# Moving the last third of a weight load to a second DMA queue in a pointwise-convolution kernel

## The chip, the cores and the metric

The kernel runs on one core of one Trainium2 chip. The metric is device time in microseconds (us), the median of several runs. "The profile" is one profiled execution of the same program; its span is counted from its first to its last instruction and is about 2 us shorter than the device time.

Engines are named as in the profile: PE is TensorE's matmul, PEld its weight load, DVE VectorE, ACT ScalarE, POOL GpSimd, SP SyncE. SPq and ACTq are the DMA issues of SyncE and ScalarE. [...]q1 is the queue of SyncE's transfers, q10 that of ScalarE's.

## The reference, cut to what matters

The input x has shape (1, 384, 384, 384), dw (1, 1, 384), pw (384, 384), all bf16.

```python
def reference(x, dw, pw):
    B, H, W, C = x.shape
    k = dw.shape[0]            # 1: no padding, no neighbours
    ...
    out = out + xp[:, i:i+H, j:j+W, :] * dw[i, j][None, None, None, :]
    return jnp.einsum('bhwc,cd->bhwd', out, pw)
```

With k = 1 each of the 147,456 pixels is a row of 384 channels, scaled by dw and multiplied by the 384 x 384 matrix pw.

## The kernel before

The scale is folded into the weights once, at the start: the kernel forms diag(dw) times pw by matmuls with scaled selection matrices (`sel_w`), which also puts the rows of pw into the order in which VectorE's 32 x 32 block transpose delivers the channels of x. The result is `w_r`. Then 288 tiles of 512 pixels each are transposed by VectorE, multiplied by TensorE (48 matmuls of 32 rows and 384 columns, four of them side by side in the array), cast by ScalarE and stored by SyncE.

The loads at the start. `pw_n` is a part of the tile `raw`, which is the name that the profile gives to it:

```python
nc.scalar.dma_start(dw_row[:], dw.rearrange("a e c -> a (e c)")).then_inc(s_dw, 16)
nc.sync.dma_start(pw_n[:, 0], pw[0:P, :]).then_inc(s_pw, 16)                       # line 178
nc.sync.dma_start(pw_n[:, 1:3], pw[P:C, :].rearrange("(k p) d -> p k d", p=P)).then_inc(s_pw2, 16)   # line 179
load_x(0)                                                                          # line 132: x0, 384 KB
# ... then x1 (384 KB), x2 and x3 (768 KB each), x4 (1536 KB), all on SyncE's queue;
# the first load of 3840 KB waits until x1 has landed
```

TensorE's program up to the main matmuls. The idle work keeps the array busy while nothing has arrived; the last third of the weights (k = 2) is multiplied twice for the same reason:

```python
idle_work(4)                                    # line 239, on constants
nc.tensor.wait_ge(s_dw, 16)
# ... three small matmuls that turn dw into a column
idle_work(2)
nc.tensor.wait_ge(s_pw, 16)
times = {(2, 0): 2, (2, 1): 2}
for k in range(3):
    if k == 1:
        nc.tensor.wait_ge(s_pw2, 16)
    nc.tensor.wait_ge(s_sw, k + 1)
    for r in range(2):
        if k == 2:
            nc.tensor.wait_ge(*w_done[r])       # PSUM free: the cast of step r is done
        for v in [0, 1] * times.get((k, r), 1):
            mm = nc.tensor.matmul(              # line 272
                PS[(k + 1) % 2][:, 2 * r + v, :D],
                lhsT=sel_w[64 * v : 64 * v + 64, k, r, :, :].rearrange("p q w -> p (q w)"),
                rhs=pw_n[64 * v : 64 * v + 64, k, :],
                start=True, stop=True, tile_position=(64 * v, 0),
            )
        mm.then_inc(s_w)
```

The six results are cast to `w_r`, the second by VectorE and the others by ScalarE (line 377, `w_out`). The main matmuls (line 222) wait for the transposed x and, in the first tile, for the casts as they need them:

```python
w_eng = [1, 0, 1, 1, 1, 1]                      # 0: VectorE, 1: ScalarE
w_first = {(0, 0): [(0, 1), (1, 3)], (4, 0): [(1, 4)], (4, 1): [(1, 5)]}
steps = [(b, par) for b in range(4) for par in range(2)] + [(4, 0), (5, 0), (4, 1), (5, 1)]
```

ScalarE's program begins with the issue of the dw load, then two small copies, then the casts:

```python
for s in range(2):
    nc.scalar.copy(warm[:, s : s + 1], nc.const_aps.tensor(0.0, [P, 1], F32)).then_inc(s_a[s])   # line 338
# ...
o = nc.vector.tensor_copy(out, in_) if e == 0 else nc.scalar.copy(out, in_)                      # line 377
```

## Time and profile before

| what | value |
|---|---|
| device time, median of 3 runs | 573.81 us (573.74 to 574.17) |
| span of the profile | 571.9 us |
| PE busy | 567.0 us (99%) |
| DVE busy | 505.4 us (88%) |
| ACT busy | 418.4 us (73%) |
| DMA, mean over the span | 397 GB/s |
| first main matmul (line 222) starts | 6.52 us |
| last main matmul of line 222 ends | 566.37 us |

A row of the groups view reads: line, engine, operation, tile written from tile read, shape, count, then busy time in us and the mean of one instruction in ns, then the idle time of the engine just before them and what ended most of it. A row of the chain view is start, length and what was running, for the chain of work that ended last. A row of the timeline is start and length in us, engine, line and operation, with the idle time ahead of it and what ended it in square brackets. A row of the DMA queues is queue, packets, MB and the time of the packets as a share of the 16 engines.

### The profile page before, as it was taken

To read this page: it belongs to the slowest core of one execution; us is meant where nothing else is said; L and a number is where in the kernel's file an instruction comes from. 1 tells how busy PE (TensorE), PEld (TensorE's weight loads), DVE (VectorE), ACT (ScalarE), POOL (GpSimd) and SP (SyncE) were. 2 spreads that over 40 slices of the span, in tenths; PEclk is the share of its full clock that TensorE was granted. 3 is DMA by queue.
4 is the path that set the end of the run, shared out by engine and by line. 5 is a ranking of instruction groups with operands and counts; after the bars stand their busy time and mean duration, and the time that the engine had idled before them with its cause. 6 is when DMAs were issued, how large, how long until landed. Compare 5 with 4: busy or idle time off the path is not lost.

```text
span 571.9 us, 29705 instructions
## 1 busy us (share of the span) xinstructions
PE 567.0 (99%) x13843; PEld 380.0 (66%) x13843; DVE 505.4 (88%) x586; ACT 418.4 (73%) x298; POOL 13.9 (2%) x41
## 2 busy tenths in 40 slices
PE   9999999999999999999999999999999999999997
PEld 4666666666666666666666666666666666666664
DVE  6889889889889889889889889889889889889885
ACT  6777777777777777777777777777777777777775
POOL 2042000000000000000000000000000000000000
PEclk9999999999999999999999999999999999999999
DMA  8999999999999999999999999999999999998677
GB/s 328 445 393 414 426 416 428 437 426 411 430 416 420 388 396 432 388 390 396 433 382 396 418 415 408 397 416 414 395 403 428 387 394 402 420 393 351 285 287 263
DMA packets 26740, 226.88 MB, mean 397 GB/s; under 512 B 1385, under 2 KB 7274, under 8 KB 22890
## 3 DMA queue, kind: packets, MB, share of 16 engines
q1 hardware_dynamic: 25796, 225.91, 97.4%
q10 hardware_dynamic: 934, 0.89, 0.4%
q14 instruction: 9, 0.07, 0.0%
q8 instruction: 1, 0.02, 0.0%
HBM read 113.54 MB, written 113.25 MB: 397 GB/s over the span
## 4 chain that ended last, share of the span: by engine, by line
PE 98%; DMA 1%; SPq 0%; DVE 0%; issue 0%; ACT 0%; POOLq 0%
PE ps L222 98%; DMA X<-in_x_dram 1%; PE ps L307 0%; PE ps L295 0%; DVE T L361 0%; ACT O L416 0%; SPq L179 0%; SPq L178 0%; SPq L457 0%; POOLq L112 0%; POOLq L446 0%
## 5 line engine op out<-in xcount | busy, mean ns | idle before, releaser
L222 PE MATMUL ps<-w_r,T 32*128 32x384 bf16 x13776 | 559.8, 321 | 0.2 <-DVE T L361 0.2
L361 DVE STREAM_TRANSPOSE T<-X 128x384 uint32<-128x384 uint32 x572 | 498.1, 874 | 58.2 <-DMA X<-in_x_dram 2.1
L421 ACT CAST O<-ps 128x1536 bf16<-128x1536 f32 x286 | 411.4, 1438 | 147.0 <-PE ps L222 147.0
L222 PEld LDWEIGHTS ps<-w_r,T 32*128 32x128 bf16 x13776 | 377.2, 93 | 183.1 <-issue 0.9
L336 POOL COPY Xk<-Xl 32x256 bf16<-32x256 bf16 x16 | 6.3, 394 | 0.0
L335 POOL COPY Xk<-Xl 32x128 bf16<-32x128 bf16 x16 | 4.6, 287 | 25.2 <-DMA Xl<-in_x_dram 24.3
L377 ACT CAST w_r<-ps 128x768 bf16<-128x768 f32 x5 | 3.6, 820 | 0.8 <-PE ps L272 0.8
L330 POOL COPY raw<-w_r 32x768 bf16<-32x768 bf16 x4 | 3.3, 819 | 6.4 <-ACT w_r L377 6.2
L239 PE MATMUL ps<-const-bfloat16-1.0 32*128 32x384 bf16 x24 | 2.2, 516 | 1.1 <-PEq L446 1.1
L272 PE MATMUL ps<-raw 64*128 64x384 bf16 x16 | 2.9, 513 | 0.1
L338 ACT ACT_TABLE_LOAD x1 | 1.3, 1283 | 1.5 <-PEq L446 1.5
L272 PEld LDWEIGHTS ps<-raw 64*128 64x128 bf16 x16 | 0.8, 113 | 2.2 <-DMA raw<-in_pw_dram 1.2
L412 DVE CAST O<-ps 128x384 bf16<-128x384 f32 x2 | 1.0, 552 | 1.4 <-PE ps L222 1.4
L361 DVE STREAM_TRANSPOSE T<-Xl 128x384 uint32<-128x384 uint32 x2 | 1.8, 876 | 0.2
L239 PEld LDWEIGHTS ps<-const-bfloat16-1.0 32*128 32x128 bf16 x24 | 0.7, 117 | 1.4 <-issue 1.4
L349 DVE STREAM_TRANSPOSE T<-Xk 128x384 uint32<-128x384 uint32 x2 | 1.2, 578 | 0.5 <-PE ps L222 0.4
L382 DVE TENSOR_REDUCE sel<-eye 128x64 f32<-128x128 bf16 x1 | 0.3, 290 | 1.5 <-POOL eye L317 1.5
L307 PE MATMUL ps<-raw,T 128*128 128x384 bf16 x8 | 1.5, 327 | 0.0
L416 ACT CAST O<-ps 128x384 bf16<-128x384 f32 x2 | 1.0, 478 | 0.7 <-PE ps L307 0.7
L377 DVE CAST w_r<-ps 128x768 bf16<-128x768 f32 x1 | 1.0, 958 | 0.5 <-PE ps L272 0.5
L416 DVE CAST O<-ps 128x384 bf16<-128x384 f32 x2 | 1.1, 558 | 0.1
L411 ACT CAST O<-ps 128x384 bf16<-128x384 f32 x2 | 0.9, 482 | 0.5 <-PE ps L222 0.5
(13 smaller groups left out, 4.5 us busy)
## 6 DMA issues: line engine op xcount, KB each, us to landing
X<-in_x_dram SPq DMA_DIRECT2D x26, 3840.0 KB, 21.9
out_dram<-O SPq DMA_DIRECT2D x26, 3840.0 KB, 27.9
X<-in_x_dram SPq DMA_DIRECT2D x3, 1536.0 KB, 18.5
out_dram<-O SPq DMA_DIRECT2D x4, 768.0 KB, 7.7
out_dram<-O SPq DMA_DIRECT2D x2, 1536.0 KB, 13.7
X<-in_x_dram SPq DMA_DIRECT2D x1, 2304.0 KB, 20.2
out_dram<-O SPq DMA_DIRECT2D x1, 2304.0 KB, 11.1
X<-in_x_dram SPq DMA_DIRECT2D x4, 384.0 KB, 4.4
```

What stands on the lines that cost most here:

```text
L222: mm = nc.tensor.matmul(PS[s][:, q, :D], lhsT=Ts[s][32 * q : 32 * q + 32, b, par::2], rhs=w_r[32 * q : 32 * q + 32, b, par, :], start=(b, ...
L239: nc.tensor.matmul(PS[0][:, 2 * (i % 2) + i // 2, :D], lhsT=ones[32 * i : 32 * i + 32, 0:P], rhs=ones[32 * i : 32 * i + 32, :], start=True ...
L272: mm = nc.tensor.matmul(PS[(k + 1) % 2][:, 2 * r + v, :D], lhsT=sel_w[64 * v : 64 * v + 64, k, r, :, :].rearrange("p q w -> p (q w)"), rhs ...
L307: mm = nc.tensor.matmul(PS[1][:, m, :D], lhsT=Tk[:, P * (m + 2) : P * (m + 3), par], rhs=w_k[:, par, :], start=False, stop=par == 1,)
L330: nc.gpsimd.tensor_copy(w_k[quads[n]], w_r[quads[n], n]).then_inc(s_wk)
L335: nc.gpsimd.tensor_copy(Xk[quads[n], g:8:4, :], x_b).then_inc(s_xk)
L336: nc.gpsimd.tensor_copy(Xk[quads[n], 8 + g : 24 : 4, :], Xl[quads[g], :, 64 * n : 64 * n + 64]).then_inc(s_xk)
L338: nc.scalar.copy(warm[:, s : s + 1], nc.const_aps.tensor(0.0, [P, 1], F32)).then_inc(s_a[s])
L361: ins = nc.vector.transpose(out=Tw[:, 3 * h : 3 * h + 3], in_=Xw[:, :, j, 96 * h : 96 * h + 96].rearrange("p k (b w) -> p b k w", w=32),)
L377: o = nc.vector.tensor_copy(out, in_) if e == 0 else nc.scalar.copy(out, in_)
L416: o = (nc.scalar.copy if n % 2 else nc.vector.tensor_copy)(Ov[:, n, j, :], PS[s][:, n, :D])
L421: a = nc.scalar.copy(Ov[:, :, j, :], PS[s][:, :, :D])
```

## The change

pw is loaded in three parts of 128 rows (96 KB each). The first two stay on SyncE's queue ahead of x0, each with a load of its own. The third is issued by ScalarE on its own queue, after ScalarE has seen the first part land. So the third part is no longer in the queue ahead of x0, and the transfer of x0 can begin that much sooner. TensorE waits for the third part with a semaphore of its own. Nothing that is computed changes.

```diff
+    s_pw3 = nc.alloc_semaphore("s_pw3")
...
         nc.sync.dma_start(pw_n[:, 0], pw[0:P, :]).then_inc(s_pw, 16)
-        nc.sync.dma_start(pw_n[:, 1:3], pw[P:C, :].rearrange("(k p) d -> p k d", p=P)).then_inc(s_pw2, 16)
+        nc.sync.dma_start(pw_n[:, 1], pw[P : 2 * P, :]).then_inc(s_pw2, 16)
         load_x(0)
...
         for k in range(3):
-            if k == 1:
-                nc.tensor.wait_ge(s_pw2, 16)
+            if k >= 1:
+                nc.tensor.wait_ge(s_pw2 if k == 1 else s_pw3, 16)
             nc.tensor.wait_ge(s_sw, k + 1)
...
         for s in range(2):
             nc.scalar.copy(warm[:, s : s + 1], nc.const_aps.tensor(0.0, [P, 1], F32)).then_inc(s_a[s])
+        nc.scalar.wait_ge(s_pw, 16)
+        nc.scalar.dma_start(pw_n[:, 2], pw[2 * P : C, :]).then_inc(s_pw3, 16)
```

## The prediction

> **What bounds the kernel now.** I read the chain of work that ended last first, because it says whether anything before the first real matmul counts. Its columns are start us, length us, what:

> ```profile
> 0.96 0.39 SPq L178
> ...
> 1.41 0.41 SPq L179
> ...
> 1.87 3.94 DMA X<-in_x_dram
> ...
> 5.84 0.59 DVE T L361
> ...
> 6.52 559.85 PE ps L222 x12053
> ```

> From 6.52 us on the chain is nothing but TensorE's main matmuls (line 222), to 566.37 us. Whatever moves that start moves the end by as much, as long as TensorE stays gapless. The groups view confirms it, and shows a second thing, the two speeds of the array:

> ```profile
> L222 PE MATMUL ps<-w_r,T 32*128 32x384 bf16 x13776 | 559.8, 321 | 0.2 <-DVE T L361 0.2
> ...
> L239 PE MATMUL ps<-const-bfloat16-1.0 32*128 32x384 bf16 x24 | 2.2, 516 | 1.1 <-PEq L446 1.1
> L272 PE MATMUL ps<-raw 64*128 64x384 bf16 x16 | 2.9, 513 | 0.1
> ```

> Line 222 idles 0.2 us in all: no later load, store or copy holds TensorE, so the change can act at the start only. Matmuls of the same 384 columns take 513 to 516 ns in the opening (lines 239, 272) and 321 ns afterwards. In the trace, successive pairs of line 272 start 320 ns apart, successive groups of four of line 222 162 ns apart: the array runs at half speed until somewhere between 5.79 us (the last slow pair) and 6.7 us.

> Next the timeline of the opening (start, length, engine, line, count, and in brackets the idle time before and what ended it):

> ```profile
> 2.83 0.28 ACT L338 COPY warm<-const-float32-0.0 128x1 f32<-128x1 f32 x2
> ...
> 3.92 0.22 PEld L272 LDWEIGHTS ps<-raw 64*128 64x128 bf16 x4 [0.42 <-DMA raw<-in_pw_dram]
> 4.23 0.96 DVE L377 CAST w_r<-ps 128x768 bf16<-128x768 f32 x1 [0.48 <-PE ps L272]
> 4.82 0.16 PEld L272 LDWEIGHTS ps<-raw 64*128 64x128 bf16 x4 [0.69 <-issue]
> ...
> 5.84 2.01 DVE L361 STREAM_TRANSPOSE T<-X 128x384 uint32<-128x384 uint32 x4 [0.65 <-DMA X<-in_x_dram]
> ```

> Two branches meet at 6.52. The x branch: x0 lands at 1.87 + 3.94 = 5.81, the first transpose ends at 6.42, the first matmul follows 0.1 later. The weight branch: pw's second load lands at 3.88 (1.41 plus the 2.5 us that the view of `raw` gives from issue to landing), k = 1 goes through TensorE from 3.92, and the eight matmuls of k = 2 start at 4.85 and 5.13, 5.45, 5.77 in pairs, so TensorE is free at 5.77 + 0.32 = 6.09. They were not waiting for pw: they waited for ScalarE's cast that frees PSUM (4.71). The x branch is last by about 0.4 us. That is all that can be won by shortening it alone.

> [...] ScalarE issued a 384 KB load at 24.32 us while SyncE's queue was full. From 28.0 to 31.5 us the view of the DMA queues reads:

> ```profile
> q1 hardware_dynamic: 47, 1.44, 102.6%
> q10 hardware_dynamic: 47, 0.07, 5.5%
> ```

> 47 packets each of q1 (SyncE) and q10 (ScalarE): strictly one to one, by packets and not by bytes. The first q10 packet started 3.84 us after the issue, while q1 packets took 1.14 us each; the alone-running dw load at 0.97 had its packet after 0.93 us. So a few packets (about (3.84 - 0.93) / 1.14 = 2.6) already queued on each engine went ahead. [...] The trace shows the halved speed and its end near 6.5 us[...].

> **The change part by part.**

> *Removed from ahead of x0:* 128 rows of 768 B, 8 packets on each of 16 DMA engines. In the trace such a packet takes 36 ns, so 8 x 36 = 0.29 us. As a check, the landings of the first load (96 KB) and the second (192 KB) are 2.97 and 3.88: 0.91 us for 16 packets per engine, half of which would be 0.45, with part of it start-up that stays. I take 0.3. x0's own issue (1.87) plus the 0.96 us that pw's packets took from issue to start allows its packets at 2.83, so the descriptors are not the limit. x0 then lands at about 5.5.

> *Added on ScalarE:* one wait and one issue. pw's first part lands at 2.97; ScalarE's copies are dispatched by 2.93, so the issue runs from about 3.0 for 0.4 to 0.55 us (its other loads: 0.42, 0.54 and 0.65) and ends before the first cast at 3.91. No cost there.

> *The moved transfer:* its packets can start at 3.0 + 0.93 = 3.9, plus about three queued x0 packets of 0.12 us: 4.0 to 4.4. By then x0 is mostly through, so the mixing gives back only one to three packets of 36 ns, about 0.07 us; x0 lands near 5.6 and the first transpose ends near 6.2. But the 8 packets per engine now alternate with x0's tail and x1's 3072 B packets (121 ns): 7 to 8 turns of 121 + 36 = 157 ns make 1.1 to 1.25 us. Last packets at about 5.1 to 5.6, plus about 0.37 us from last packet to semaphore (x0 in the trace: last completion write near 5.45, landed 5.81), plus some spread over 16 engines: pw's third part lands at about 6.0, between 5.4 and 6.4.

> *On TensorE:* k = 2 now starts at about 6.05 and not 4.85. Its four slots of 320 ns cost 1.28 us, so the main matmuls start at 7.3 if the array is still slow, +0.8; with 160 ns slots at 6.7, +0.2. The casts behind them stay hidden: cast 4 ends about 1.7 us and cast 5 about 2.4 us after the landing, while line 222 wants them at step 8 and step 10 of its first tile, 1.28 + 8 x 0.16 = 2.6 and 2.9 us after it.

> *The clock:* TensorE now stands idle from about 4.6 to 6.05. [...]

> **Rivals.** (1) *The author's intent holds:* the third part lands by 5.0, as an unhindered 2.0 us load would, k = 2 is done by 6.2, and the shorter x branch is all that counts: -0.2 to -0.3, 573.5. For it: at 4 us x0 leaves gaps, and there were wide ones around 3.6 us in the DMA record. Against: the one-to-one turns and the 3.84 us seen at 24.32. (2) *The wait for pw takes the place of the wait for x0,* clock unharmed: +0.2 to +0.8, 574.0 to 574.6. This I think likeliest. (3) *The same with a late clock:* about +2, 576. For it: the speed-up came so near 6.5 in this trace. Against: [...]the three times before (573.74 to 574.17) show no run that paid much for it. (4) *The third part waits behind x2 and x3 too* (6144 B and 12288 B rows, 0.23 us and more a turn): landing near 7.5 to 8, +2 to +3. Against: x2's packets started only at about 5.7.

> **Range and chances.** About one in seven for (1), nearly one half for (2), a third for (3), the rest for (4). The middle of this is +0.7: 574.5 us. Eight in ten lie between 573.5 (rival 1) and 576.2 (rival 3). 2% would be 11.5 us, more than the whole opening up to the first main matmul is long (6.52 us), so the verdict of the three chances is all but settled: faster 0.005, within 2% 0.98, slower 0.015.

> **What would show it.** In the changed profile: x0's DMA piece ends near 5.6 and not 5.81; a second idle entry of line 272 that ends with the DMA of pw, about 1.2 us longer than before; line 222 starts at 6.7 to 7.3, with the chain of work leading through ScalarE's issue and pw's transfer rather than through x0; ScalarE's first cast still near 3.9. If line 222's first tiles take 3.9 us each and not 1.95, the clock was late. I am wrong if pw's third part lands before 5.0, if line 222 starts before 6.5, or if x0 lands no earlier than before.

## The result and the profile after

The changed kernel takes 579.38 us (median of 6 runs, 578.28 to 581.24) against 573.89 us before (6 runs, 573.74 to 574.17): a ratio of 1.0099 with a 95% interval of 1.0083 to 1.0115. It is slower by 5.5 us. The prediction had 574.5 us, with 573.5 to 576.2 as its range.

The chain of work that ended last, in the changed kernel (start us, length us, what; its lines are one further down in the file, so line 223 is the old 222, 273 the old 272):

```profile
2.96 6.48 DMA raw<-in_pw_dram
...
9.48 1.46 PE ps L273 x8
10.95 561.04 PE ps L223 x13776
```

Before, the chain ran through x0's transfer (to 5.81) and reached the main matmuls at 6.52. Now it runs through the moved third of pw: issued at 2.96, landed at 9.44. Both parts of the loss stand here. The main matmuls start 10.95 - 6.52 = 4.43 us later, and they take 561.04 - 559.85 = 1.19 us longer: 5.62 of the 5.7 us by which the spans differ (577.6 and 571.9).

The groups view tells who waits now (after the bar: busy us, mean ns, then idle us and what ended most of it):

```profile
L223 PE MATMUL ps<-w_r,T 32*128 32x384 bf16 x13776 | 561.1, 321 | 0.0
L273 PE MATMUL ps<-raw 64*128 64x384 bf16 x16 | 2.9, 516 | 4.7 <-DMA raw<-in_pw_dram 4.7
```

Line 223 still has no idle time, so its extra 1.19 us are slower matmuls and not gaps. The opening's timeline, for the times of x0 and of the issue:

```profile
2.96 0.37 ACTq L341 DMA_DIRECT2D raw<-in_pw_dram  x1
...
3.91 2.20 ACT L380 CAST w_r<-ps 128x768 bf16<-128x768 f32 x3 [0.80 <-PE ps L273]
...
5.79 1.97 DVE L364 STREAM_TRANSPOSE T<-X 128x384 uint32<-128x384 uint32 x4 [0.60 <-DMA X<-in_x_dram]
9.48 0.13 PEld L273 LDWEIGHTS ps<-raw 64*128 64x128 bf16 x4 [5.34 <-DMA raw<-in_pw_dram]
```

The first transpose starts at 5.79; it was 5.84. So the purpose of the change, an earlier x0, was reached by 0.05 us, and k = 2 waits for its weights: 5.34 us at TensorE's weight load, 4.7 us at its matmuls.

What moved in between? Packets per queue in two stretches of the changed kernel (q1 SyncE, q10 ScalarE; packets, MB, share of the engines), first 4.0 to 5.7 us, in which the queue of ScalarE isn't listed at all:

```profile
q1 hardware_dynamic: 241, 0.69, 102.2%
```

and 6.3 to 7.5 us:

```profile
q1 hardware_dynamic: 73, 0.44, 90.5%
q10 hardware_dynamic: 64, 0.05, 12.0%
```

For nearly two us after they should have begun, none of the third's packets moved: the engines were full with x0 and x1, and then with the first of x2. The first of its 128 packets of 768 B came at 5.81 us, its 16 completions from 8.19 to 9.44. From 6.3 to 7.5 us the queues took turns nearly one to one (73 and 64 packets), but x2 was on the other side by now, whose packets are 0.44 MB / 73 = 6 KB long and take 234 ns.

### The profile page after: what moved, and what is told of

Its sections match the earlier page's. It is cut to its first block, busy times and chain, and to the rows that moved or that the text cites. A ratio compares the mean times of both kernels' runs of the same rounds, so it can differ in the third digit from the quotient of the medians.

```text
span 577.6 us, 29706 instructions
## 1 busy us (share of the span) xinstructions
PE 568.2 (98%) x13843; PEld 340.1 (59%) x13843; DVE 509.1 (88%) x586; ACT 418.4 (72%) x298; POOL 13.9 (2%) x41
## 4 chain that ended last, share of the span: by engine, by line
PE 98%; DMA 1%; ACT 0%; ACTq 0%; issue 0%; POOLq 0%
PE ps L223 97%; DMA raw<-in_pw_dram 1%; PE ps L273 0%; PE ps L308 0%; ACT L339 0%; PE ps L296 0%; ACTq L178 0%; ACT O L419 0%; ACT warm L339 0%; ACTq L460 0%; POOLq L113 0%; POOLq L449 0%
## 5 line engine op out<-in xcount | busy, mean ns | idle before, releaser
L223 PEld LDWEIGHTS ps<-w_r,T 32*128 32x128 bf16 x13776 | 337.4, 93 | 223.9 <-issue 1.9
## 6 DMA issues: line engine op xcount, KB each, us to landing
out_dram<-O SPq DMA_DIRECT2D x1, 2304.0 KB, 11.6
```

What stands on the lines that cost most here:

```text
L223: mm = nc.tensor.matmul(PS[s][:, q, :D], lhsT=Ts[s][32 * q : 32 * q + 32, b, par::2], rhs=w_r[32 * q : 32 * q + 32, b, par, :], start=(b, ...
```

## The experiments

Theory A, formed from these lines: (1) what an engine has already been given by the other queue goes first; (2) then each packet of the third pays one packet of the other queue; (3) the idle gap leaves the array at half speed for the first main matmuls. Rivals: a fixed start-up of some 3 us for a load of ScalarE's (B), a strict order of issue (C, O), or a cost of splitting the load. "L" is the landing of pw's last third in the profiled run, "main" the start of the main matmuls.

**Only the split.** All three parts on SyncE's queue ahead of x0.

```diff
+        nc.sync.dma_start(pw_n[:, 2], pw[2 * P : C, :]).then_inc(s_pw3, 16)     # behind the second part
-        nc.scalar.wait_ge(s_pw, 16)
-        nc.scalar.dma_start(pw_n[:, 2], pw[2 * P : C, :]).then_inc(s_pw3, 16)
```

> One part of the change alone: pw's second and third parts as loads of their own, both still on SyncE's queue ahead of x0, nothing on ScalarE. Theory A (all of the loss is the move to the second queue): x0 issued 0.45 us later but still behind the same packets, landing near 5.8 to 5.9, main matmuls at 6.5 to 6.6: 573.9 us, within 0.3 of before. Rival: splitting the load itself costs, about 0.4 us (the added issue), 574.3.

Measured: 574.45 us (13 runs), ratio 1.0006, interval 0.9998 to 1.0015. k = 2 starts at 4.86, as before. The split costs about 0.3 us by the ratio, and 0.9 us at the upper end of the interval; the loss of 5.5 us is not the split's.

**x2 held back** until the third has landed.

```diff
+            if f is load_x and a == (2,):
+                nc.sync.wait_ge(s_pw3, 16)
```

> The changed kernel, with SyncE issuing x2 (and what follows) only when pw's last third has landed. In the changed kernel the first packets of the third came at about 5.8 to 6.6 us and then took turns with x2's 234 ns packets. Theory A (packets that SyncE's queue has already handed to each DMA engine go first, here x0's and x1's 16; then one to one): first packets still near 5.5 to 5.8, but then nothing beside them, so that it lands near 6.3; main matmuls start near 7.6, about 575.0 us, more if the clock is late. Theory C (ScalarE's descriptors are made only after those of x2, which SyncE issued 0.1 us earlier): with x2 gone the packets start near 4.2 and mix with x0 and x1, landing near 5.8, main matmuls at 7.1, 574.5 us. Theory B (a load of ScalarE takes about 3 us to start whatever is queued) expects the same as A here; the next run tells them apart.

Measured: 576.64 us, ratio 1.0043 (1.0029 to 1.0057). The queues from 4.0 to 5.2 us, and the chain:

```profile
q1 hardware_dynamic: 170, 0.47, 102.3%
```

```profile
2.92 3.80 DMA raw<-in_pw_dram
...
6.77 1.46 PE ps L275 x8
8.23 560.65 PE ps L225 x13274
```

Again nothing of q10 until x0 and nearly all of x1 were through (first packets from 5.27 us), though x2 wasn't there: theory C, which had them start near 4.2, falls. Without x2 beside it L is 6.73 and not 9.44, so the turns with x2 were worth 2.7 us. The time is 1.6 us above A's figure: L came 0.4 later, and the main matmuls ran at half speed until 10.0 (26 matmuls from 8 to 10 us, 56 from 10 to 12), which A had named but not counted.

**x1 held back** as well: the same edit with `a == (1,)`.

> The changed kernel, with SyncE issuing x1 (and what follows) only when pw's last third has landed; only x0 is then queued ahead of it. Theory A (queued packets go first, then turns): first packets near 4.5, landing near 5.3, x0 still near 5.75, main matmuls at about 6.6, 573.9 us (573.6 to 574.4). Theory B (a fixed 3 us until ScalarE's load starts): packets near 5.9, landing near 6.4, main matmuls at 7.7, 575 us. Theory C (descriptors behind x2's): packets near 4.1, landing near 5.0, 573.8 us.

Measured: 576.23 us, 1.0035 (1.0023 to 1.0046). From 4.3 to 5.3 us the queues read:

```profile
q10 hardware_dynamic: 144, 0.10, 31.4%
q1 hardware_dynamic: 47, 0.10, 24.3%
```

The third moves as soon as x0 is nearly through, from 4.3 us, 1.4 us after its issue at 2.88, and L is 5.6. So a fixed start-up of 3 us (B) falls. A's places in time nearly hold (first packets from 4.3 for 4.5, L 5.6 for 5.3), its time doesn't: main starts at 7.05 and the first main matmuls are slow until 9.6 (36 matmuls from 8 to 10 us, 56 from 10 to 12). In this run pw's second part landed late too, at 4.21.

**Issued later**, behind ScalarE's fourth cast, when x2, x3 and x4 have been issued too.

```diff
-        nc.scalar.wait_ge(s_pw, 16)
-        nc.scalar.dma_start(pw_n[:, 2], pw[2 * P : C, :]).then_inc(s_pw3, 16)
...
             o.then_inc(s_wr[e])
+            if i == 3:
+                nc.scalar.dma_start(pw_n[:, 2], pw[2 * P : C, :]).then_inc(s_pw3, 16)
```

> The changed kernel, with ScalarE issuing pw's last third only behind its fourth cast, near 5.3 us, when SyncE has issued x2, x3 and x4 as well. It tells two readings of the late start apart. Theory O (a transfer is served behind whatever the other queue issued earlier; only issues that overlap in time are mixed): the packets come behind x4's, landing near 14, main matmuls near 15.5, about 584 us. Theory A (a limited stock of packets already fetched by each engine, some 60 to 80 KB by the two starts seen so far, goes first; then turns one to one): first packets near 8.5 to 9.5 in the midst of x3, turns with x3's 234 ns and x4's 460 ns packets, landing near 12, main matmuls near 13.3, about 582 us.

Measured: 583.65 us, 1.0167 (1.015 to 1.0184), nearer to O's number. But the trace has A's mechanism. Chain, and the queues from 8.2 to 9.2 us:

```profile
4.79 8.18 DMA raw<-in_pw_dram
...
13.02 1.46 PE ps L273 x8
14.48 561.57 PE ps L223 x13208
```

```profile
q1 hardware_dynamic: 65, 0.39, 92.6%
q10 hardware_dynamic: 35, 0.03, 9.1%
```

The packets came from 8.26 us on, in the midst of x3 (0.39 MB / 65 = 6 KB each) and before x4's, and L is 12.97: not "behind everything issued earlier". The time is 1.7 us above A's 582: L came a us later, the main matmuls began at 14.4 for 13.3, and the array stayed slow until 18.1 us. The clock record of this trace shows it directly (windows view: stretch, length, PE busy and matmuls, ..., granted clock, DMA share, GB/s):

```profile
16.00:18.20 2.20, 2.20 (x36) 1.07 (x32) 0.86 (x1) 0.00 (x0) 2.03 (x4) 0.51 1.00 433
18.20:20.00 1.80, 1.80 (x52) 1.08 (x48) 1.49 (x2) 1.44 (x1) 0.79 (x1) 1.00 0.99 419
```

36 matmuls in 2.2 us at a clock of 0.51, 52 in 1.8 us at 1.00.

**x2 issued after the third**, by 16 fulfilled waits ahead of it, but still long before x1 is through.

```diff
+            if f is load_x and a == (2,):
+                for _ in range(16):
+                    nc.sync.wait_ge(s_pw, 16)
```

> The changed kernel, with SyncE passing 16 more waits on pw's first part (long fulfilled) before it issues x2, so that x2 is issued at about 3.5 us, half a us after ScalarE's issue and not 0.14 us before it; x2 is still ready on its queue long before x1 is through. Theory O (order of issue decides): the third part goes right behind x1 as a block, ahead of x2, landing near 6.5, main matmuls near 7.8, about 575.9 us. Theory A in its plain form (turns between queues that have work, at the moment of service): x2's packets are there by then too, so turns as in the changed kernel, landing near 9, about 579 us.

Measured: 577.26 us, 1.006 (1.0044 to 1.0077). From 5.5 to 6.2 us:

```profile
q1 hardware_dynamic: 42, 0.13, 86.5%
q10 hardware_dynamic: 124, 0.08, 38.4%
```

The third goes as a block right behind x1, and L is 6.98 (O's 6.5). The time lies between O's and A's; the trace decides. The half us between the two issues mattered, so A's second part has to be put more exactly. One reading fits both this run and the late issue (where O fails): the order of the packets was settled some time before they moved. Here x2, issued at 3.44 us, still came behind the third, whose packets moved from 5.5 to 6.2; there the third's first packets moved ahead of x4's, which had been issued earlier. From issue to first packet it was 2.9 us in the changed kernel (2.96 to 5.81) and 3.5 us in the late issue (4.79 to 8.26). That reading is inferred: the traces show when packets move, and not when or where their order is settled.

**Smaller packets beside it:** x2 as two loads of 384 KB.

```diff
-    head, tail = [[1, 1, 2, 2, 4]], [[6, 4], [4, 1, 1, 1, 1]]
+    head, tail = [[1, 1, 1, 1, 2, 4]], [[6, 4], [4, 1, 1, 1, 1]]
```

> The changed kernel, with the 768 KB load x2 split into two loads of 384 KB, whose packets are 3072 B (121 ns) as those of x0 and x1 and not 6144 B (234 ns). Theory A (pw's last third pays one packet of the other queue for each of its own 8): from a start near 6, 8 turns of 157 ns and not 270: landing near 7.6 to 8.2 and not 9.4, main matmuls near 9.2, about 577.7 us, 1.7 below the changed kernel. Rival (it is the late start alone): landing as before near 9.4, 579.4 us.

Measured: 578.22 us, 1.0079 (1.0058 to 1.0101). The chain:

```profile
2.91 4.92 DMA raw<-in_pw_dram
...
7.88 1.16 PE ps L273 x8
9.04 561.05 PE ps L223 x13120
```

The packets again start near 5.9, and L is 7.83 and not 9.44: as A has it, and the rival (the late start alone) falls. The trace decides this; the four times (577.39 to 579.93) overlap those of the changed kernel.

**More packets:** the third as two loads of 192 columns each, with the wait at 32.

```diff
-        nc.scalar.dma_start(pw_n[:, 2], pw[2 * P : C, :]).then_inc(s_pw3, 16)
+        for h in range(2):
+            cols = slice(192 * h, 192 * h + 192)
+            nc.scalar.dma_start(pw_n[:, 2, cols], pw[2 * P : C, cols]).then_inc(s_pw3, 16)
```

> The changed kernel, with pw's last third as two loads of 192 columns: the same bytes in twice as many packets, 16 and not 8 on each DMA engine. Theory A (the queues take turns by packets, one to one): 16 turns of 0.234 + 0.03 us next to x2's and x3's packets, so that the landing goes from 9.4 to about 11.6 and the time up by about 2.2 us, to about 581.6. Rival D (shared by bytes, or a late start alone): landing within 0.5 us of 9.4, time within 0.6 us of 579.4.

Measured: 582.68 us (580.26 to 584.08), 1.0155 (1.0134 to 1.0176), 3.3 above the changed kernel; A had 2.2, D nothing. The profiled run was the lowest of the four, 580.26, with L at 9.80; in it the first half slipped in ahead of x2 and only the second took turns. So the times speak for A, but the trace that would show 16 turns is not there, and the second half was also issued 0.4 us later (at 3.29), which may be part of the loss.

**TensorE kept busy** while it waits, by 18 rounds of idle matmuls into the half of PSUM that k = 2 overwrites.

```diff
+        def idle_work(n, s=0):                          # s: the half of PSUM that it writes
...
+            if k == 2:
+                nc.tensor.wait_ge(*w_done[0])
+                nc.tensor.wait_ge(*w_done[1])
+                idle_work(18, 1)
```

> The changed kernel with 18 rounds of idle matmuls (4 each, into the PSUM half that the k = 2 products later overwrite) put between k = 1 and the wait for pw's last third, so that TensorE is busy while it waits. It measures the clock's share by itself. Theory A (of the 5.5 us, about 4.4 are the late landing of pw's last third at 9.44 and about 1.2 the array at half speed in the first main matmuls): the landing stays at about 9.4, the k = 2 pairs take 160 ns each and not 320, the main matmuls start near 10.1 and not 10.95 and take 559.9 us and not 561.0: about 577.3 us, 2.0 below the changed kernel. Rival B (the array is slow for another reason than the gap, or the gap costs nothing): main matmuls start near 10.9, time within 0.3 us of 579.4.

Measured: 579.01 us (577.77 to 581.01), 1.0085 (1.0056 to 1.0115): no clear gain. The chain tells why:

```profile
2.98 8.07 DMA raw<-in_pw_dram
...
11.10 0.82 PE ps L277 x8
11.92 559.76 PE ps L223 x13776
```

The clock's share is gone as A has it: k = 2 takes 0.82 us and not 1.46, the main matmuls 559.76 and not 561.04, together 1.92 us. But L was 11.05 in this run, 1.6 later. L varies from run to run (the six times of the changed kernel have a spread of 3 us, the six before beside them of 0.4), so the total can't show 1.9 us here.

**The same where L doesn't depend on turns:** x2 held back, 5 rounds of idle work.

> The kernel that holds x2 back until pw's last third has landed (576.64 us, landing 6.7), with 5 rounds of idle matmuls while TensorE waits. Nothing else moves beside the third part there, so its landing doesn't change from run to run, and the clock's share can be read in the time. Theory A: the array is at full speed when the third part lands, the k = 2 pairs are 160 ns apart (0.6 us less) and the main matmuls lose nothing (0.9 us in the profile of the kernel without the idle work): 575.1 us, 1.5 below. Rival: the gap costs nothing, 576.6 us.

Measured: 576.07 us (575.34 to 576.83), 1.0036 (1.0022 to 1.005), against 576.64 (576.31 to 576.82) without the idle work. The chain:

```profile
7.12 0.76 PE ps L279 x8
7.88 4.01 PE ps L225 x96
11.89 0.36 issue
12.25 556.10 PE ps L225 x13680
```

k = 2 runs at full speed (0.76 us) and the main matmuls do so from the first (56 matmuls from 8 to 10 us, 26 without the idle work), but they now come so early that the held-back x2 (landed at 11.19) is late: a gap of 0.36 us after the second tile. 0.6 of the expected 1.5 us is left, and the intervals of the two ratios overlap. So the clock's 1.2 us in the changed kernel is shown by the traces, and the times only point the same way. That L stays the same from run to run with x2 held, no run shows.

**ScalarE issues at once**, right behind dw, without waiting.

```diff
         nc.scalar.dma_start(dw_row[:], dw.rearrange("a e c -> a (e c)")).then_inc(s_dw, 16)
+        nc.scalar.dma_start(pw_n[:, 2], pw[2 * P : C, :]).then_inc(s_pw3, 16)
...
-        nc.scalar.wait_ge(s_pw, 16)
-        nc.scalar.dma_start(pw_n[:, 2], pw[2 * P : C, :]).then_inc(s_pw3, 16)
```

> The changed kernel, with ScalarE issuing pw's last third right after dw, near 1.5 us, without waiting for the first part to land. Theory A (what counts is how many packets are queued on the engines when ScalarE's arrive): they arrive near 2.4, when pw's first part has nearly gone, so the third lands near 3.8 to 4.2, before k = 2 wants it (4.85); x0 lands near 5.8; main matmuls start near 6.5, 573.9 us (573.6 to 574.2). Theory B (a load of ScalarE takes about 3 us to start beside a busy SyncE queue): packets near 4.5, landing near 6, main matmuls near 7.3, 574.7 us.

Measured: 574.09 us (13 runs), ratio 0.9999 (0.9991 to 1.0007). The same load on the same queue, issued 1.4 us earlier, costs nothing: L is 4.15, and the chain is x0's again:

```profile
1.87 4.21 DMA X<-in_x_dram
...
6.78 559.83 PE ps L224 x13776
```

**One queue, behind x0:** SyncE issues x0, then the third, then x1.

```diff
         load_x(0)
+        nc.sync.dma_start(pw_n[:, 2], pw[2 * P : C, :]).then_inc(s_pw3, 16)
...
-        nc.scalar.wait_ge(s_pw, 16)
-        nc.scalar.dma_start(pw_n[:, 2], pw[2 * P : C, :]).then_inc(s_pw3, 16)
```

> What the change meant to do, on one queue: pw's last third issued by SyncE between x0 and x1. Theory A (behind x0 is too late in any case, but in one queue it lands right behind x0): x0 near 5.6, the third near 5.9 to 6.1, k = 2 done 1.28 us later, main matmuls at 7.2 to 7.4, 574.7 us, and up to 1.3 us more if the clock is late. Rival (behind x0 is early enough and only the second queue was at fault): third near 5.3, main matmuls at 6.5 or before, 573.5 to 573.9 us.

Measured: 575.67 us, 1.0028 (1.0017 to 1.0038). In the profile the rival's steps came true: x0 lands at 5.13, L is 5.43, main starts at 6.26, 0.26 earlier than before. The time was lost behind that:

```profile
2.82 5.76 DMA X<-in_x_dram
...
9.33 2.13 PE ps L224 x48
...
11.55 555.96 PE ps L224 x13680
```

Now x1 is the chain, landing at 2.82 + 5.76 = 8.58 (before: 6.78), and the second tile starts late. In the trace six of the 16 engines finish x1 between 8.16 and 8.59 us and nine by 6.56, and single reads of x1 took 0.6 to 1.6 us. All eight times (575.06 to 576.34) lie above the median before, so the loss is not one run's chance; what makes x1 late in this order was not tried.

**Another order:** ScalarE issues the second part behind dw, SyncE the first part, x0, the third part, x1.

> A try at a better order from the same reading: ScalarE issues pw's second part right after dw (near 1.5 us, when SyncE's queue holds little), SyncE issues the first part, then x0 at 1.41, then the third part, then x1. Theory A: second part near 3.7 to 4.1, x0 near 5.0 to 5.4, third part near 5.2 to 5.6, main matmuls between 6.2 and 6.9, 573.5 to 574.2 us. Rival (x0's last engines land near 5.8 whatever goes ahead of it, as in both kernels so far): no gain, 573.9 us or more.

Measured: 576.12 us, 1.0032 (1.0019 to 1.0044); here x0 came early, at 4.85, and now the second part was late:

```profile
1.53 3.53 DMA raw<-in_pw_dram
...
5.11 2.10 PE ps L274 x12
7.29 561.30 PE ps L224 x13776
```

ScalarE issued it at 1.53, SyncE had issued x0 at 1.41: it moved behind and among x0's packets and landed at 5.06; TensorE stood idle 0.9 us for it. The same thing at another place. No kernel tried here beats the one before.

## Why the prediction was wrong

The step that failed is the start of the moved transfer: "plus about three queued x0 packets of 0.12 us: 4.0 to 4.4". The changed kernel showed the first packets at 5.8 to about 6.6 us instead, beside x2 and not x1. Three was a count of packets, (3.84 - 0.93) / 1.14 = 2.6, taken where each was 30,720 B, and carried over to packets of 3,072 B. In bytes those 2.9 us were 360 GB/s x 2.9 us / 16 = 65 KB per engine (GB/s from the windows view). The same sum, an estimate, from issue + 0.93 us to the first packets gives 47 to 66 KB for the changed kernel (395 and 389 GB/s, first packets taken as 5.8 to 6.6 us on the different engines), and 66 to 90 KB for the late issue (415 and 391 GB/s, 8.3 to 9.3 us). So what went first was, by this estimate, some 50 to 90 KB per engine in all three; in the changed kernel all that was left of x0, all of x1 and some of x2. By count of packets the three don't agree (2.6 against more than ten). Whether bytes or time set it can't be told here, since the engines moved 360 to 415 GB/s in all three, and no run shows what holds the third back.

From that the rest followed. Rival (4), the third waiting behind x2, was put aside because "x2's packets started only at about 5.7": the third's started at 5.8. Its size was too small as well, since I gave it a landing of 7.5 to 8; eight turns of 0.27 us and the spread over the engines led to 9.44.

Of the prediction's three signs of being wrong none appeared: two look for a third or a main start that comes early, the last for an x0 that is no earlier (it was, by 0.05 us), and none for a late landing.

The other steps one by one:

- *x0 sooner by 0.3 us, 0.2 net:* 0.05 measured. The median engine's x0 landed 0.14 earlier (5.17 to 5.03 in the trace), but the last of 16 counts, and three engines were at 5.51 to 5.76. In the ten profiles that have x0 behind two thirds of pw and the last third behind x0, the last engine's landing is 4.96 to 5.81, in the middle 5.5, which is the 0.3 I had; but with all thirds ahead it was 5.81, 5.55 and 6.08 in three profiles. The scatter of single slow reads is as large as the gain.
- *ScalarE's issue is free:* right. At 2.96 for 0.37 us, the first cast still at 3.91.
- *One-to-one turns:* right, 73 against 64 packets, each of them a single row (768 B against 6,144 B). It is the partner that was wrong, 234 ns for 121.
- *k = 2 costs 1.28 us:* 1.40 from its first matmul (9.48) to the first main one (10.88), 1.46 in the chain. Nearly right. The casts stayed hidden: line 223 has no idle time.
- *A late clock, about +2 us in all at a chance of one in three:* it came, with 1.19 us in the main matmuls. The size was my estimate; the trace before did not show how long the array stays slow after a gap. In the traces of both kernels (the stretches of 3.41 us are worked out in the last section) the kernel before held 3.12 us of matmuls (91%) in the stretch before its clock rose at 6.60; the changed kernel held 1.46 us in 3.30 to 6.71 (43%), 0.65 us in the next 3.41 us, and rose at 13.54 only. That the size came so close (about 2 less rival (2)'s 0.8) is partly luck: the same loss was 0.80 us with x2 held and 1.72 us in the late issue.
- *The move carries to the end one to one:* right. 4.43 + 1.19 makes up the span's difference.

## What to carry to other kernels

In these runs a second DMA queue is not a side road: the packets of a load issued on it at 2.96 or 4.79 us came 2 to 3 us late, behind what the other queue moved meanwhile (an estimated 50 to 90 KB on each engine), and then paid about one of the other queue's packets for each of its own (73 against 64). So a small load with short rows that something waits for is issued before the large ones (at 1.53 us it cost nothing, at 2.96 us 5.5 us); if it must come later, hold back the large loads or give them short packets (L 6.73 and 7.83 for 9.44). And a wait on the way to a TensorE-bound loop can cost more than its length: here the array came out of it at half speed, for 0.8 to 1.7 us more.
